# Filling small column tiles over six rounds, making the first matrices in one go with a repeated product, and putting the inverses' endings behind the next products

## The chip, the core and the metric

The kernel runs on one core of a Trainium2 chip. The metric is device time in microseconds (us) of one execution. Engines are named as the profile names them: PE (TensorE, matrix products, with PEld for its weight loads), DVE (VectorE), ACT (ScalarE), POOL (GpSimd) and SP (SyncE, which only issues DMAs here). DMAs are also issued from POOL's and ACT's queues. Each engine works through its own instructions in order; waits between engines are semaphores that the tile framework sets from the tiles that instructions read and write.

## The reference

Two independent computations, joined along the last axis. Part A is an attention layer that goes over 64 segments of 32 positions, each with the 8 memory rows that the segment before it left. Part B, the one that this change touches, is a state space convolution:

```python
dt = jnp.exp(log_dt)[:, None]
logdA = dt * (A_re + 1j * A_im)
P = jnp.exp(logdA[:, :, None] * l[None, None, :])
K = jnp.einsum('dn,dnl,dn->dl', Cc, P, dB).real      # D = 1024 channels, N = 128, L = 2048
Kf = rfft(pad(K, L)); Uf = rfft(pad(u, L))           # length 2 L
y = irfft(Uf * Kf)[:, :, 0:L]
out_B = transpose(y) + u * Dskip
```

Part A, per segment s, with the weights Wq, Wk, Wv (1024 x 32 x 128 each) and Wo:

```python
h = concat([mem, x[:, s*32:(s+1)*32]])
p = softmax(mask(q k^T * scale)); o = (p v) Wo
mem = o[:, :8]; out = o[:, 8:]
```

## The kernel before

Part B comes first and part A after it. Part B has four stages.

**Table rounds.** A loop over `f` from -1 to 16 makes the kernel values K. Sixteen rounds r of channels pass through it; round r is begun in iteration r and ended in iteration r+1. In a round PE makes the exponents (`pa`) and the phases (`ptt`), ACT takes the exponentials (`E0` to `E7`, in a buffer `E`), then the sines (`S`) and cosines (`C`) of both halves, DVE moves phases (`n`), takes absolute values (`b`), negates (`w`) and forms the products `gi` and `gr`, and PE multiplies these into the kernel values (`K`, tile `kp`), which DVE writes into the tile `KxT` (`x`). The order of these steps is a list of words written by hand, `ORDER`, and `LAST` for f = 16; a word with a prime belongs to the round before. ACT changes its table between the exponentials and the sines once per round each way.

Beside the rounds run side operations, at places that the list names: `P`, projections of weights (tile `pro`); `U`, the forward transform of u: PE makes `ups`, ACT copies one as `ua`, DVE forms sum and difference `us` (L974, L975), POOL combines these into `ux` (L979 to L982) and stores it to the DRAM table `Ud` (L983); `M`, transposes of the transform's matrices, `mt`, evicted into `ms` (L946) and stored by POOL to `MId` (L947). A side operation runs in one place and is evicted (`run_evict`) at a later one.

**Columns of turns.** The matrices G of the kernel's spectrum are sines of angles that are products of two small factors, `lhs` (7 rows, 1408 columns) and `rhs` (7 rows, 2048 columns), and a weight factor `wts`. Their transposed columns, `g_l` and `g_r`, are filled in `columns_of_turns` by some forty small instructions of POOL (iota, memset, affine_select) and DVE (shifts, masks, casts), all called ahead of the round f = 3; DVE and POOL read each other's results there. In round 15 `turned_columns` transposes them on PE into tiles `gt` (30 transposes in four groups) in the slots of the side operation `P`, and ACT and DVE copy them to `lhs`, `wts` and `rhs`.

**Passage.** `build` is a generator that makes one block of G in 14 steps: one product and sine for a basis, five pairs of products with a sine each, three products with a copy (the amplitudes, into `amp`), five more pairs with a sine. In f = 16 the step `G0` does nine steps of `build(0, ...)` and `G2` the other five. `weighted` multiplies part of G by the amplitudes on DVE, and `spectrum(b, n)` (L1171) multiplies G with the kernel values `k` in 20 products of 128x256. After the rounds, the last kernel values are stored to the DRAM table `Kd` from `KxT`, in DMAs dealt out to SP and POOL in turn. `make(kc, n)` does steps of the three other blocks.

**Product loop.** For b = 0 to 15, `pointwise(b)` multiplies the spectra of u (`uq`, loaded from `Ud` by SP) by those of the kernel (in PSUM) into `z` and `y` (four multiplies, L1366), then adds and subtracts (L1369, L1370) and writes `Bt` (L1372). It is a generator with a stop behind the multiplies; between its two halves the loop issues the products of spectrum b+1. From b = 4 on, each iteration runs two inverses. An inverse is 32 products into `yp` (and one more of 4 rows for one kind), an eviction by ACT into `yb` (L1438), a multiply of `uu` by `Dsk` and an addition of `yb` on DVE (L1441, L1442) and a DMA of `uu` to the output from ACT's queue (L1443), which is held back in the list `unsent` until a later inverse. The tile `uu` is loaded by SP six inverses ahead, into nine buffers. The product tiles of the spectra, `hps`, have three buffers. Eight inverses are left for a tail behind the loop, in which the resident weights of part A are loaded too.

Part A streams most of its weights (`wst`) from DRAM in every segment.

The lines that set the order around the change:

```python
LAST = ("w0' b0' C0' b1' gi0' C1' G0 gr0' w1' gr1' gi1' K0' K1' G1 x0' x1' G2 M0 G3 m0").split()
for f in range(-1, 17):
    if f == 3:
        columns_of_turns()
```

Of the kernel before, what the change touches and what calls it, by code (L numbers as in the profile page):

```python
# [10 lines left out]
BF16 = mybir.dt.bfloat16  # L11
# [651 lines left out]
def part_b(ctx, tc, u, A_re, A_im, B_re, B_im, C_re, C_im, log_dt, Dskip, out_b, ahead, copies, residents, first_state):  # L663
# [32 lines left out]

    g_l = tabs.tile([128, 14, 7], BF16, name="g_l")
    g_r = tabs.tile([128, 4, 4, 7], BF16, name="g_r")
    par_t = [tabs.tile([128, 8, 128], BF16, name="pt%d" % n_) for n_ in range(2)]
# [222 lines left out]
    tmp = ctx1.enter_context(tc.tile_pool(name="b_tmp", bufs=2))  # L922
    up = ctx1.enter_context(tc.tile_pool(name="b_up", bufs=1, side="right"))
    ctx_p = ctx.enter_context(ExitStack())
    ps_t = ctx_p.enter_context(tc.tile_pool(name="b_pst", bufs=2, space=PSUM))
# [116 lines left out]
    def columns_of_turns():  # L1042

        at = tabs.tile([128, 6], I32, name="g_at")
        for j, (b0, step) in enumerate(((0, 2), (256, 2), (512, 4), (1024, 8), (2048, 16), (0, 2))):
            gp.iota(at[:, j:j + 1], pattern=[[1, 1]], base=b0, channel_multiplier=step)
        atF = tabs.tile([128, 6], F32, name="g_atF")
        v.tensor_copy(out=atF[:], in_=at[:])

        def select(t_, dims, fill, base, cm):  # L1050
            gp.affine_select(out=t_, in_=t_, compare_op=ALU.is_ge, fill=float(fill), base=base, pattern=[[0, n_] for n_ in dims], channel_multiplier=cm)
        for j, fill in ((2, 513), (3, 1025), (4, 2050)):
            select(atF[:, j:j + 1], (1,), fill, -1, 1)
        select(atF[:, 5:6], (1,), 1, 4, -1)
        select(atF[:, 5:6], (1,), 3, 5, -1)
        v.tensor_copy(out=at[:], in_=atF[:])
        hl = tabs.tile([128, 2, 6], I32, name="g_hl")
        v.tensor_scalar(out=hl[:, 0, :], in0=at[:], scalar1=6, scalar2=None, op0=ALU.logical_shift_right)
        v.tensor_scalar(out=hl[:, 1, :], in0=at[:], scalar1=63, scalar2=None, op0=ALU.bitwise_and)
        for i, (lo, n_) in enumerate(((0, 2), (2, 3))):  # L1060
            v.tensor_copy(out=g_l[:, 0:10, lo:lo + n_].rearrange("p (s j) c -> p s j c", s=2),
                          in_=hl[:, i, 0:5].unsqueeze(1).unsqueeze(3).to_broadcast([128, 2, 5, n_]))
            v.tensor_copy(out=g_l[:, 10, lo:lo + n_], in_=hl[:, i, 5:6].to_broadcast([128, n_]))
        gp.memset(g_l[:, 0:11, 5:6], 1.0)
        gp.memset(g_l[:, 0:11, 6:7], 0.25)
        gp.memset(g_l[:, 5:10, 6:7], 0.0)
        pn = tabs.tile([128, 4], I32, name="g_pn")
        gp.iota(pn[:, 0:1], pattern=[[1, 1]], base=0, channel_multiplier=1)
        v.tensor_scalar(out=pn[:, 1:2], in0=pn[:, 0:1], scalar1=1, scalar2=None, op0=ALU.bitwise_and)
        v.tensor_scalar(out=pn[:, 2:3], in0=pn[:, 0:1], scalar1=4, scalar2=None, op0=ALU.logical_shift_right)  # L1070
        v.tensor_scalar(out=pn[:, 3:4], in0=pn[:, 0:1], scalar1=15, scalar2=None, op0=ALU.bitwise_and)
        pnF = tabs.tile([128, 5], F32, name="g_pnF")
        v.tensor_copy(out=pnF[:, 0:4], in_=pn[:])
        gp.memset(g_l[:, 11:14, :], 0.0)
        gp.memset(g_l[:, 11:14, 0:1], 1.0)
        gp.memset(g_l[:, 12:14, 1:2], 2.0)
        gp.memset(g_l[:, 13:14, 2:4], 2.0)
        for i, j in ((0, 1), (1, 2), (2, 4)):
            v.tensor_scalar(out=g_l[:, 11 + i, j:j + 1], in0=pnF[:, 1:2], scalar1=-2.0, scalar2=2.0, op0=ALU.mult, op1=ALU.add)
        select(g_l[:, 11:13, 0:5], (2, 5), 0, -1, 1)  # L1080
        select(g_l[:, 13:14, 4:5], (1, 1), 0, -1, 1)
        gp.memset(g_l[:, 11:13, 5:6], 2.0)
        gp.memset(g_l[:, 12:13, 6:7], 2.0)
        select(g_l[:, 11:13, 5:7], (2, 2), 0, 0, -1)
        kq = tabs.tile([128, 2, 16], I32, name="g_kq")
        gp.iota(kq[:, 0, :], pattern=[[1, 4], [0, 4]], base=0, channel_multiplier=0)
        gp.iota(kq[:, 1, :], pattern=[[0, 4], [1, 4]], base=0, channel_multiplier=0)
        kqF = tabs.tile([128, 2, 16], F32, name="g_kqF")
        v.tensor_copy(out=kqF[:], in_=kq[:])
# [6 lines left out]
        gp.memset(g_r[:, :, :, 5:6], 128.0)  # L1096
        gp.memset(g_r[:, :, :, 6:7], 1.0)

    G = {}

    def turned_columns():

        for i in range(4):
            pt = take([128, 8, 128], BF16, "gt")
            for c in range(8 if i != 1 else 6):
                pe.transpose(out=pt[0:7, c, :], in_=g_l[:, 8 * i + c, :] if i < 2 else g_r[:, 2 * (i - 2) + c // 4, c % 4, :], identity=ident[:])

            def evict(copy, i=i, pt=pt):
                flat = pt[0:7].rearrange("p c n -> p (c n)")
                if i == 0:  # L1110
                    copy(out=G["lhs"][:, 0:1024], in_=flat)
                elif i == 1:
                    copy(out=G["lhs"][:, 1024:1408], in_=flat[:, 0:384])
                    copy(out=G["wts"], in_=flat[:, 384:768])
                else:
                    copy(out=G["rhs"][:, 1024 * (i - 2):1024 * (i - 2) + 1024], in_=flat)
            yield evict

# [147 lines left out]
    for eng, names in ((sc.copy, ON_ACT), (v.tensor_copy, ON_DVE)):  # L1266
        for nm, kind, slot in names:
            evict_of[nm] = (kind, slot, eng)
    LAST = ("w0' b0' C0' b1' gi0' C1' G0 gr0' w1' gr1' gi1' K0' K1' G1 x0' x1' G2 M0 G3 m0").split()
    for f in range(-1, 17):  # L1270
        if f == 3:
            columns_of_turns()
        if f == 15:
# [7 lines left out]
            G.update({0: part_of(g0, 0), "rhs": g0[0:7, 5120:7168], "wts": g0[0:7, 7168:7552], "basis": g0[0:7, 7552:8064], "lhs": k0[0:7, 2560:3968]})  # L1281
            side_ops["P"] = (turned_columns(),)
        if f == 16:
# [3 lines left out]
        for word in ORDER if f < 16 else LAST:  # L1287
            nm, r = word.rstrip("'"), f - word.endswith("'")
            if f == 16 and nm[0] in "GMm" and not word.endswith("'"):
                if nm == "G0":  # L1290
                    for _ in range(9):
                        next(made)
                elif nm == "G1":
                    weighted(0, 0, amp0)
                elif nm == "G2":
                    for _ in made:
                        pass
                    s0 = ps_e.tile([128, 2, 512], F32, name="pa", tag="pa")
# [15 lines left out]
            elif nm in evict_of:  # L1314
                run_evict(*evict_of[nm])
                if f == 15 and nm == "m":
                    run_evict("U", 3, v.tensor_copy)
            elif nm[0] in side_ops:
# [6 lines left out]
            elif 0 <= r <= 15:  # L1325
                table_ops[nm[:-1]](r, int(nm[-1]))
                if f == 15 and nm == "x1":
                    run_side("U", 3)
    for n_, f_ in enumerate(late):
        f_((sy, gp)[n_ % 2])  # L1330
# [95 lines left out]
    def inverse(dq, c, uu, neg, mn):  # L1426
# [11 lines left out]
        sc.activation(out=yb[:], in_=yp, func=ACT.Copy, scale=float(2.0 / PLEN))  # L1438
        while len(unsent) > (1 if len(todo) > 6 else 0):
            unsent.pop(0)()  # L1440
        v.tensor_tensor(out=uu[:], in0=uu[:], in1=Dsk[:, d].unsqueeze(1).to_broadcast([128, 2, DQ]), op=ALU.mult)  # L1441
        v.tensor_tensor(out=uu[:], in0=uu[:], in1=yb[:], op=ALU.add)  # L1442
        unsent.append(lambda: sc.dma_start(out=out_v[r][:, mc:mc + 2, d], in_=uu[:]))  # L1443

# [13 lines left out]
    for b in range(16):  # L1458
# [3 lines left out]
        points = pointwise(b, now)  # L1462
        next(points)
        if b == 0:
            ctx_p.close()
# [46 lines left out]
    for n_ in range(3):  # L1512
        inverse_begin(3, 2 * n_, begun[n_ // 2][:, n_ % 2])
    ctx2.close()
    for n_ in range(8):
        inverses(1)
        for _ in range((9, 5)[n_] if n_ < 2 else 1):
            next(resident, None)
# [161 lines left out]
```

## Time and profile before

| what | us |
|---|---|
| median of 3 runs | 2044.19 (2042.81 to 2046.65) |
| profiled execution | 2047.62 |
| its span in the profile | 2045.9 |
| table rounds end (ACT's last exponential table) | about 424 |
| first multiply of `pointwise(0)` starts | 466.94 |
| product loop in a steady period (b = 4 on) | 13.07 each |
| part A's PE work starts | about 697 |

Mean granted TensorE clock: 0.975. The bytes moved are 588.69 MB, at a mean of 288 GB/s. A row of a timeline has the start, the length, the engine, the line, the operation, output and inputs, and in brackets the engine's idle time before it and the instruction that ended it. A row of a group has the total busy time and the mean of one in ns, then the idle time before the group's instructions and its main releaser. A line number is that of the kernel before. "PEclk" is the granted clock as a share of the full one.

### The profile page before, as it was taken

The page shows a single profiled execution, that of the slowest core. Times are in us where ns is not written, and L with a number is a line of the kernel's source. Part 1 is how long each engine was busy: PE and PEld are TensorE (multiplying, and loading weights), DVE is VectorE, ACT ScalarE, POOL GpSimd, SP SyncE. Part 2 cuts the span into 40 slices and gives each one's busy share as a digit, 9 for nine tenths or more (in the row PEclk, how much of TensorE's full clock was granted, in tenths as well). Part 3 has the DMA queues.
Part 4 walks back from the last instruction along what each step waited for, and adds up shares of the span by engine and source line. Part 5 has one row for each costly group of instructions (what it writes and reads, how often), then busy time and mean ns, then how long its engine had stood idle before and what let it go on. Part 6 is the DMA issues. An engine that isn't in the chain of part 4 may idle for free.

```text
span 2045.9 us, 74541 instructions
## 1 busy us (share of the span) xinstructions
PE 1834.5 (90%) x31928; PEld 1130.4 (55%) x31956; DVE 1411.2 (69%) x3442; ACT 958.1 (47%) x1672; POOL 415.3 (20%) x851
## 2 busy tenths in 40 slices
PE   1698999866999879999999999999999999999998
PEld 1365666644877535555555555555555555555554
DVE  8878999958887346666766667666666666666650
ACT  4887988862222324443444444444434444344430
POOL 2135454442200011111111111111111111111121
PEclk9999999977999979999999999999999999999999
DMA  6787997746446999999999999999999999999991
GB/s 169 185 227 227 274 269 202 200 139 212 158 141 203 316 325 339 340 341 340 344 348 332 339 335 358 344 343 344 350 325 350 342 339 341 345 347 344 345 339 50
DMA packets 348469, 588.69 MB, mean 288 GB/s; under 512 B 109865, under 2 KB 225913, under 8 KB 346089
## 3 DMA queue, kind: packets, MB, share of 16 engines
q1 hardware_dynamic: 294748, 526.35, 76.0%
q10 hardware_dynamic: 44812, 28.26, 4.5%
q0 software_dynamic: 8576, 29.32, 4.0%
q8 instruction: 250, 4.10, 0.8%
q14 instruction: 83, 0.67, 0.1%
HBM read 528.25 MB, written 66.05 MB: 290 GB/s over the span
## 4 chain that ended last, share of the span: by engine, by line
PE 35%; DMA 24%; DVE 4%; issue 1%; ACT 1%; POOL 0%; SPq 0%; POOLq 0%; DVEq 0%; ACTq 0%
PE acc L375 18%; DMA wst<-WD_v 11%; PE pp L488 9%; DMA wst<-WD_o 5%; DMA arena<-PKd 3%; PE pe L625 3%; PE tr L386 2%; DMA wst<-WD_q 2%; DMA wst<-WD_k 2%; PE pv L456 1%; PE pv L460 1%; DVE arena L582 1%; ACT arena L582 1%; PE sc L400 1%; PE tro L588 1%
## 5 line engine op out<-in xcount | busy, mean ns | idle before, releaser
L375 PEld LDWEIGHTS <-a_hT 128*32 128x32 bf16 x12352 | 327.2, 96 | 318.3 <-issue 63.0
L381 ACT CAST arena<-acc 128x512 bf16<-128x512 f32 x384 | 224.7, 585 | 397.6 <-PE acc L375 321.9
L375 PE MATMUL acc<-W,a_hT 128*32 128x512 bf16 x4608 | 334.7, 380 | 2.2 <-issue 1.2
L488 PEld LDWEIGHTS <-arena 128*32 128x32 bf16 x8256 | 216.8, 97 | 86.3 <-issue 62.5
L375 PE MATMUL acc<-wst,a_hT 128*32 128x512 bf16 x2304 | 229.7, 381 | 26.6 <-DMA wst<-WD_v 17.8
L389 POOL COPY arena<-arena 128x128 bf16<-128x128 bf16 x128 | 37.4, 292 | 851.4 <-DMA arena<-PKd 300.3
L296 DVE TENSOR_SCALAR arena<-keep 128x256 int32<-128x256 int32 (+1 forms) x512 | 175.5, 394 | 28.1 <-PE acc L375 26.8
L375 PE MATMUL acc<-gF,a_hT 128*32 128x512 bf16 x2048 | 145.6, 382 | 0.0
L488 PE MATMUL pp<-W_o,arena 128*32 128x256 bf16 x4096 | 139.0, 275 | 6.4 <-DMA W_o<-in_A_Wo_dram 5.1
L168 PE MATMUL pro<-xTl,wsl 128*128 128x512 bf16 x490 | 115.9, 389 | 16.2 <-ACT kst L177 7.9
L415 DVE TENSOR_REDUCE a_mx<-sc 128x4 f32<-128x160 f32 (+1 forms) x192 | 71.6, 373 | 77.5 <-PE sc L403 77.5
L419 ACT ACTIVATE sc<-sc 128x160 f32<-128x160 f32 (+1 forms) x192 | 63.9, 333 | 122.9 <-DVE sc L416 122.1
L503 DVE COPY arena<-tr 128x512 bf16<-128x512 bf16 x64 | 27.2, 425 | 128.3 <-PE tr L386 128.3
L423 DVE TENSOR_REDUCE a_mx<-sc 128x4 f32<-128x160 f32 (+1 forms) x192 | 72.8, 379 | 55.5 <-ACT sc L419 55.1
L1208 ACT ACTIVATE E<-pa 128x648 bf16<-128x648 f32 x128 | 90.9, 710 | 32.2 <-PE pa L1200 27.0
L1423 PE MATMUL yp<-Bt,MI 128*128 128x256 bf16 x680 | 104.6, 273 | 0.7 <-ACT yb L1438 0.7
L450 POOL TENSOR_TENSOR arena<-arena,a_BD 128x128 bf16<-128x128 bf16 x128 | 51.0, 399 | 234.9 <-DVE arena L433 218.5
L168 PEld LDWEIGHTS <-wsl 128*128 128x128 bf16 x512 | 51.1, 100 | 77.7 <-issue 23.3
L582 ACT CAST arena<-pp 128x128 bf16<-128x128 f32 x64 | 17.0, 265 | 161.3 <-DVE arena L582 161.3
L375 PE MATMUL acc<-W_v,a_hT 128*32 128x512 bf16 x1280 | 92.3, 381 | 0.0
L1216 DVE TENSOR_SCALAR nr<-ptt 128x456 f32<-128x456 int16 x128 | 77.3, 624 | 17.7 <-PE ptt L1194 16.0
L386 PEld LDWEIGHTS <-arena 128*128 128x128 bf16 x1024 | 57.8, 98 | 54.5 <-issue 44.9
(311 smaller groups left out, 3866.5 us busy)
## 6 DMA issues: line engine op xcount, KB each, us to landing
wst<-WD_v SPq DMA_DIRECT2D x256, 512.0 KB
wst<-WD_k SPq DMA_DIRECT2D x192, 512.0 KB
wst<-WD_o SPq DMA_DIRECT2D x192, 512.0 KB
wst<-WD_q SPq DMA_DIRECT2D x128, 512.0 KB
Ud<-ux POOLq DMA_DIRECT2D x16, 1024.0 KB, 6.1
uq<-Ud SPq DMA_DIRECT2D x32, 512.0 KB
wsl<-in_A_Wk_dram SPq DMA_DIRECT2D x16, 512.0 KB
wsl<-in_A_Wv_dram SPq DMA_DIRECT2D x16, 512.0 KB
```

What stands on the lines that cost most here:

```text
L168: nc.tensor.matmul(a[:], lhsT=w[:, kc, 128 * j:128 * j + 128], rhs=xTl[:, kc, :, :].rearrange("p s k -> p (s k)"), start=(kc == 0), stop=( ...
L296: nc.vector.tensor_scalar(out=out.bitcast(I32), in0=in_.bitcast(I32), scalar1=0, scalar2=None, op0=ALU.bitwise_or)
L375: nc.tensor.matmul(a[32 * g:32 * g + 32, o_:o_ + rhs.shape[1]], lhsT=hT[:, kc, :], rhs=rhs, start=(kc == 0), stop=(kc == KC - 1), tile_pos ...
L381: nc.scalar.copy(out=q, in_=a[:])
L386: nc.tensor.transpose(out=p[:, hl, :, :].rearrange("p a b -> p (a b)"), in_=q[:, 128 * hl:128 * hl + 128], identity=ident[:])
L415: nc.vector.tensor_reduce(out=m_, in_=x, axis=AX.X, op=ALU.max)
L419: nc.scalar.activation(out=flat(sc, i), in_=flat(sc, i), func=ACT.Exp, scale=scale)
L423: nc.vector.tensor_reduce(out=m_, in_=x, axis=AX.X, op=ALU.add)
L488: nc.tensor.matmul(po[32 * qt:32 * qt + 32, o_:o_ + rhs.shape[1]], lhsT=oT[:, h % 4, (h % 16) // 4, :], rhs=rhs, start=False, stop=(h == 3 ...
L1208: sc.activation(out=T["E", r, e // 4][:, lo:lo + 8 * NE].rearrange("p (i c) -> p i c", i=2), in_=T.pop(("p", r, e))[:, :, 0:4 * NE], func= ...
L1216: v.tensor_scalar(out=T["n", r, e // 4][:, lo:lo + 8 * NT], in0=T.pop(("t", r, e))[:, 0:8 * NT].bitcast(I16)[:, 0:16 * NT:2], scalar1=floa ...
L1423: pe.matmul(yp[:, b, :], lhsT=m_[:, b, cs, kc, :], rhs=Bt[:, kc, j, half, c_, :], start=(kc == 0 and cs == 0 and half == 0), stop=(kc == 3 ...
```

## The change

It has five parts.

1. `g_l`, `g_r` and the small tiles of `columns_of_turns` move from the pool `tabs` to the pool `up`, on the other side of the memory. Tiles allocated after them shift, and so does what later pools lay over the memory of earlier tiles.
2. `columns_of_turns` becomes a generator with six steps, one at the start of each of the rounds f = 1 to 6.
3. `turned_columns` no longer runs in the slots of `P`: a step is called after each of E1 to E6 of round 15, and its copies are issued with the transposes, the left ones on DVE, the right ones on ACT in halves of 512 columns.
4. In `LAST`, `G0` does all fourteen steps of `build(0, ...)`, and PE makes a product of 128x512 into a spare tile, which nothing reads, after each step. The eviction of the last `U` operation, with the POOL work and the store to `Ud` that follow it, moves from the end of round 15 to behind `x1'` of `LAST`.
5. The end of an inverse (the two DVE instructions on `uu`, and the entry in `unsent`) is put into a list, and runs after the next iteration's four multiplies; all of `unsent` is sent after the next inverse's eviction. In the tail it runs right after its inverse.

```diff
-    g_l = tabs.tile([128, 14, 7], BF16, name="g_l")
-    g_r = tabs.tile([128, 4, 4, 7], BF16, name="g_r")
...
     up = ctx1.enter_context(tc.tile_pool(name="b_up", bufs=1, side="right"))
+    g_l = up.tile([128, 14, 7], BF16, name="g_l")
+    g_r = up.tile([128, 4, 4, 7], BF16, name="g_r")
...
     def columns_of_turns():
...
+        gp.memset(g_r[:, :, :, 6:7], 1.0)
+        yield
         v.tensor_copy(out=atF[:], in_=at[:])
...
+            v.tensor_scalar(out=g_l[:, 11 + i, j:j + 1], in0=pnF[:, 1:2], scalar1=-2.0, scalar2=2.0, op0=ALU.mult, op1=ALU.add)
+        yield
         for j, fill in ((2, 513), (3, 1025), (4, 2050)):
             select(atF[:, j:j + 1], (1,), fill, -1, 1)
...
         select(g_l[:, 13:14, 4:5], (1, 1), 0, -1, 1)
+        yield
         rv = g_r[:].rearrange("p k q c -> p (k q) c")
...
+        yield
+        v.tensor_copy(out=at[:], in_=atF[:])
+        v.tensor_scalar(out=hl[:, 0, :], in0=at[:], scalar1=6, scalar2=None, op0=ALU.logical_shift_right)
+        v.tensor_scalar(out=hl[:, 1, :], in0=at[:], scalar1=63, scalar2=None, op0=ALU.bitwise_and)
+        yield
+        for i, (lo, n_) in enumerate(((0, 2), (2, 3))):
...
+        yield
...
-            def evict(copy, i=i, pt=pt):
...
-                    copy(out=G["rhs"][:, 1024 * (i - 2):1024 * (i - 2) + 1024], in_=flat)
-            yield evict
+            flat = pt[0:7].rearrange("p c n -> p (c n)")
+            if i == 0:
+                v.tensor_copy(out=G["lhs"][:, 0:1024], in_=flat)
+            elif i == 1:
+                v.tensor_copy(out=G["lhs"][:, 1024:1408], in_=flat[:, 0:384])
+                v.tensor_copy(out=G["wts"], in_=flat[:, 384:768])
+            else:
+                for h in range(2):
+                    sc.copy(out=G["rhs"][:, 1024 * (i - 2) + 512 * h:1024 * (i - 2) + 512 * h + 512], in_=flat[:, 512 * h:512 * h + 512])
+                    yield
+                continue
+            yield
...
-    LAST = ("w0' b0' C0' b1' gi0' C1' G0 gr0' w1' gr1' gi1' K0' K1' G1 x0' x1' G2 M0 G3 m0").split()
+    LAST = ("w0' b0' C0' b1' gi0' C1' G0 gr0' w1' gr1' gi1' G1 K0' x0' K1' x1' U3 G2 M0 G3 m0").split()
+    steps = columns_of_turns()
     for f in range(-1, 17):
-        if f == 3:
-            columns_of_turns()
+        if 1 <= f <= 6:
+            next(steps)
...
-            side_ops["P"] = (turned_columns(),)
+            turning = turned_columns()
...
-            if f == 16 and nm[0] in "GMm" and not word.endswith("'"):
+            if f == 16 and nm == "U3":
+                run_evict("U", 3, v.tensor_copy)
+            elif f == 16 and nm[0] in "GMm" and not word.endswith("'"):
                 if nm == "G0":
-                    for _ in range(9):
-                        next(made)
+                    spare = ps_t.tile([128, 512], F32, name="ptt", tag="ptt")
+                    for _ in made:
+                        pe.matmul(spare[:], lhsT=ident[:], rhs=MF[:, 0, 0:2].rearrange("p c s n -> p (c s n)"), start=True, stop=True)
                 elif nm == "G1":
                     weighted(0, 0, amp0)
                 elif nm == "G2":
-                    for _ in made:
-                        pass
...
                 run_evict(*evict_of[nm])
-                if f == 15 and nm == "m":
-                    run_evict("U", 3, v.tensor_copy)
...
                     run_side("U", 3)
+                elif f == 15 and nm in ("E1", "E2", "E3", "E4", "E5", "E6"):
+                    next(turning)
...
-        while len(unsent) > (1 if len(todo) > 6 else 0):
+        while unsent:
             unsent.pop(0)()
-        v.tensor_tensor(out=uu[:], in0=uu[:], in1=Dsk[:, d].unsqueeze(1).to_broadcast([128, 2, DQ]), op=ALU.mult)
-        v.tensor_tensor(out=uu[:], in0=uu[:], in1=yb[:], op=ALU.add)
-        unsent.append(lambda: sc.dma_start(out=out_v[r][:, mc:mc + 2, d], in_=uu[:]))
+
+        def ending():
+            v.tensor_tensor(out=uu[:], in0=uu[:], in1=Dsk[:, d].unsqueeze(1).to_broadcast([128, 2, DQ]), op=ALU.mult)
+            v.tensor_tensor(out=uu[:], in0=uu[:], in1=yb[:], op=ALU.add)
+            unsent.append(lambda: sc.dma_start(out=out_v[r][:, mc:mc + 2, d], in_=uu[:]))
+        endings.append(ending)
+
+    endings = []
+
+    def end():
+        while endings:
+            endings.pop(0)()
...
         next(points)
+        end()
...
     ctx2.close()
+    end()
     for n_ in range(8):
         inverses(1)
+        end()
```

More of the change, by code (lines that the diff above doesn't have):

```diff
@@ L1042, in columns_of_turns, with select @@
     def columns_of_turns():
-        at = tabs.tile([128, 6], I32, name="g_at")
+        def select(t_, dims, fill, base, cm):
+            gp.affine_select(out=t_, in_=t_, compare_op=ALU.is_ge, fill=float(fill), base=base, pattern=[[0, n_] for n_ in dims], channel_multiplier=cm)
+        at, pn, kq, hl = (up.tile([128, *dims], I32, name="g_%s" % nm) for nm, dims in (("at", (6,)), ("pn", (4,)), ("kq", (2, 16)), ("hl", (2, 6))))
+        atF, pnF, kqF = (up.tile([128, *dims], F32, name="g_%sF" % nm) for nm, dims in (("at", (6,)), ("pn", (5,)), ("kq", (2, 16))))
@@ L1045, in columns_of_turns @@
         for j, (b0, step) in enumerate(((0, 2), (256, 2), (512, 4), (1024, 8), (2048, 16), (0, 2))):
             gp.iota(at[:, j:j + 1], pattern=[[1, 1]], base=b0, channel_multiplier=step)
[L1047 to L1051, printed above, removed]
+        gp.iota(pn[:, 0:1], pattern=[[1, 1]], base=0, channel_multiplier=1)
@@ new lines, in columns_of_turns @@
+        gp.iota(kq[:, 0, :], pattern=[[1, 4], [0, 4]], base=0, channel_multiplier=0)
+        gp.iota(kq[:, 1, :], pattern=[[0, 4], [1, 4]], base=0, channel_multiplier=0)
+        gp.memset(g_l[:, 0:11, 5:6], 1.0)
+        gp.memset(g_l[:, 0:11, 6:7], 0.25)
+        gp.memset(g_l[:, 5:10, 6:7], 0.0)
+        gp.memset(g_l[:, 11:14, :], 0.0)
+        gp.memset(g_l[:, 11:14, 0:1], 1.0)
+        gp.memset(g_l[:, 12:14, 1:2], 2.0)
+        gp.memset(g_l[:, 13:14, 2:4], 2.0)
+        gp.memset(g_l[:, 11:13, 5:6], 2.0)
@@ new lines, in columns_of_turns @@
+        gp.memset(g_l[:, 12:13, 6:7], 2.0)
+        select(g_l[:, 11:13, 5:7], (2, 2), 0, 0, -1)
+        gp.memset(g_r[:, :, :, 5:6], 128.0)
+        gp.memset(g_r[:, :, :, 6:7], 1.0)
+        yield
+        v.tensor_copy(out=atF[:], in_=at[:])
+        v.tensor_scalar(out=pn[:, 1:2], in0=pn[:, 0:1], scalar1=1, scalar2=None, op0=ALU.bitwise_and)
+        v.tensor_scalar(out=pn[:, 2:3], in0=pn[:, 0:1], scalar1=4, scalar2=None, op0=ALU.logical_shift_right)
+        v.tensor_scalar(out=pn[:, 3:4], in0=pn[:, 0:1], scalar1=15, scalar2=None, op0=ALU.bitwise_and)
@@ L1052, in columns_of_turns @@
+        v.tensor_copy(out=pnF[:, 0:4], in_=pn[:])
+        v.tensor_copy(out=kqF[:], in_=kq[:])
+        for i, j in ((0, 1), (1, 2), (2, 4)):
+            v.tensor_scalar(out=g_l[:, 11 + i, j:j + 1], in0=pnF[:, 1:2], scalar1=-2.0, scalar2=2.0, op0=ALU.mult, op1=ALU.add)
+        yield
         for j, fill in ((2, 513), (3, 1025), (4, 2050)):
@@ L1055, in columns_of_turns @@
         select(atF[:, 5:6], (1,), 3, 5, -1)
[L1056 to L1079, printed above, removed]
         select(g_l[:, 11:13, 0:5], (2, 5), 0, -1, 1)
         select(g_l[:, 13:14, 4:5], (1, 1), 0, -1, 1)
[L1082 to L1089, printed above, removed]
+        yield
         rv = g_r[:].rearrange("p k q c -> p (k q) c")
@@ L1095, in columns_of_turns @@
         v.tensor_scalar(out=rv[:, :, 4], in0=kqF[:, 1, :], scalar1=1.0 / 8, scalar2=0.0, op0=ALU.mult, op1=ALU.add)
-        gp.memset(g_r[:, :, :, 5:6], 128.0)
-        gp.memset(g_r[:, :, :, 6:7], 1.0)
+        yield
[4 more added lines that the diff above has]
+        for i, (lo, n_) in enumerate(((0, 2), (2, 3))):
+            v.tensor_copy(out=g_l[:, 0:10, lo:lo + n_].rearrange("p (s j) c -> p s j c", s=2),
+                          in_=hl[:, i, 0:5].unsqueeze(1).unsqueeze(3).to_broadcast([128, 2, 5, n_]))
+            v.tensor_copy(out=g_l[:, 10, lo:lo + n_], in_=hl[:, i, 5:6].to_broadcast([128, n_]))
+        yield
     G = {}
@@ L1106, in turned_columns @@
                 pe.transpose(out=pt[0:7, c, :], in_=g_l[:, 8 * i + c, :] if i < 2 else g_r[:, 2 * (i - 2) + c // 4, c % 4, :], identity=ident[:])
-            def evict(copy, i=i, pt=pt):
[L1109 to L1115, printed above, removed]
-                    copy(out=G["rhs"][:, 1024 * (i - 2):1024 * (i - 2) + 1024], in_=flat)
-            yield evict
+            flat = pt[0:7].rearrange("p c n -> p (c n)")
[10 more added lines that the diff above has]
+            yield
     def sine_of(out, bank):
```

## The prediction

> **What bounds the kernel now.** I read the busy shares first, then the groups of instructions around each edit, then the timelines of single engines at the four places that the diff touches, and last the waits of the loop that follows. The span is 2045.9 us, the profiled execution 2047.62 us (1.72 outside the span), which is 3.43 above the median of 2044.19. A change of the sum is taken off the median. No engine is full over the whole span, so each stage has to be read by itself:
>
> ```profile
> PE 1834.5 (90%) x31928; PEld 1130.4 (55%) x31956; DVE 1411.2 (69%) x3442; ACT 958.1 (47%) x1672; POOL 415.3 (20%) x851
> ```
>
> The recurrent part fills 697 to 2046 us and is not in the diff. The diff lies in the table rounds (to 424 us), the passage to the products (424 to 473), the product loop (473 to 665) and its tail.
>
> First place, the round in which the columns are filled. Groups on ACT and DVE from 157 to 172 us (the last field is idle time and what ended it):
>
> ```profile
> L1230 ACT ACTIVATE nr<-nr,hp 128x1824 bf16<-128x1824 f32 x2 | 3.5, 1808 | 5.6 <-DVE nr L1227 5.6
> ...
> L1089 DVE CAST g_kqF<-g_kq 128x32 f32<-128x32 int32 x1 | 0.2, 180 | 1.0 <-POOL g_kq L1087 1.0
> L1056 DVE CAST g_at<-g_atF 128x6 int32<-128x6 f32 x1 | 0.2, 172 | 1.0 <-POOL g_atF L1051 1.0
> L1048 DVE CAST g_atF<-g_at 128x6 f32<-128x6 int32 x1 | 0.2, 171 | 1.6 <-POOL g_at L1046 1.6
> ```
>
> DVE and POOL hand small tiles to each other, DVE stands still for 3.6 us of it, and ACT, which sets the pace of the rounds, waits 5.55 us for the cosine's angles behind that.
>
> Second place, the passage. Timelines of ACT, POOL, PE and DVE (start, length, instruction, idle time before it and its end):
>
> ```profile
> 435.09 1.51 ACT L1142 CAST amp<-gf 128x512 bf16<-128x512 f32 x3
> 441.80 2.56 ACT L1120 ACTIVATE g<-gf 128x512 bf16<-128x512 int16 x5 [5.20 <-PE gf L1129]
> ```
>
> ```profile
> 429.47 2.12 POOL L980 TENSOR_TENSOR ux<-us 128x512 f32<-128x512 f32 x1
> 431.55 5.20 POOL L982 TENSOR_TENSOR ux<-us 128x256 f32<-128x256 f32 x4
> 437.16 0.57 POOL L983 DMA_DIRECT2D Ud<-ux  x1 [0.41 <-POOL ux L982]
> 450.16 0.56 POOL L947 DMA_DIRECT2D MId<-ms  x1 [12.43 <-ACT ms L946]
> ```
>
> ```profile
> 441.16 2.31 PE L1129 MATMUL gf<-g,k 7*128 7x256 bf16 x10
> 443.40 4.45 PE L1171 MATMUL pa<-k,g 128*128 128x256 bf16 x20
> 447.64 1.06 PE L942 MATMUL mt<-b_ident,MF 128*128 128x128 bf16 x8
> 448.49 2.76 PE L1171 MATMUL ptt<-k,g 128*128 128x256 bf16 x20
> ```
>
> ```profile
> 444.38 0.96 DVE L1151 TENSOR_TENSOR g<-g,amp 128x1536 bf16<-128x1536 bf16 x1 [2.55 <-ACT g L1120]
> 466.94 1.22 DVE L1366 TENSOR_TENSOR z<-uq,pa 128x1024 f32<-128x1024 f32 x1 [21.60 <-DMA Kd<-KxT]
> ```
>
> The first matrices are made in two parts, 5.20 us apart. Both spectra are ready at 451.2, but the first multiply waits to 466.94, for the kernel table's last stores: its tile z lies in the memory of KxT, which they read.
>
> Third place, the product loop. PE and DVE in one period (13.07 us, 524.64 to 537.71):
>
> ```profile
> 537.71 2.35 PE L1171 MATMUL hps<-k,gF 128*128 128x256 bf16 x20
> 541.28 2.36 PE L1171 MATMUL hps<-k,gF 128*128 128x256 bf16 x20 [1.22 <-DVE y L1366]
> ```
>
> ```profile
> 538.54 0.43 DVE L1442 TENSOR_TENSOR uu<-uu,yb 128x512 bf16<-128x512 bf16 x1 [2.14 <-ACT yb L1438]
> 538.88 1.21 DVE L1366 TENSOR_TENSOR z<-uq,hps 128x1024 f32<-128x1024 f32 x1
> ```
>
> DVE stands before the ending's addition until the inverse is evicted, and the multiplies that free PE's product buffer are queued behind it.
>
> **The change part by part.**
>
> *Columns over six rounds.* ACT's sine tables load at 135.07, 155.04 and 181.64: a round is 19.97, the one with the columns 26.60, 6.6 too long. The same steps come in six pieces, each POOL result read a round later, so the waits go. What is left on DVE is some twenty instructions of 0.15 to 0.25 us, 3.6 us, beside a slack of about 0.46 per round (0.23 before each of two steps waiting on ACT). I leave 0.8 (0 to 2). Gain 5.8, range 4.5 to 6.6.
>
> *Transposes and columns' copies in round 15.* Before, PE does them at 402 to 404 in an idle time that lasts to 412. Now they are queued after E1 to E6. DVE meets the first copy (7x1024, about 0.98 by ACT's row of that shape) after `pa` of E1, which PE starts at 412.12, and the second after E2's eight `ups` products, at about 416.6, ahead of wn, gr1 and gi1 in its order. So gi1, ending at 415.58 before, ends about 421.2; the kernel products that read it stand at 418.17, and go to about 421.3. ACT loses two 0.98 copies and gains four halves between its E evictions. This is a cost of 4 (0.5 if DVE takes the wait in the 1.1 it stands idle later and the rest of the round closes up, 5 if all of it is passed on).
>
> *First matrices in one go, with a repeated product.* ACT's fourteen steps are 2.95 + 1.51 + 2.56 = 7.0 us. From 432.23 they would end at 439.3, where before they end at 444.3. The product after each step is 128x512: at the half clock of 430 to 445 (granted 0.50) about 0.43, beside 0.46 for a step's own two. At 0.9 to 1.0 a step PE is slower than ACT's 0.5. The rows show how long that lasts: PE works without a gap from 443.40, and only the second spectrum (2.76 against 4.45) sees the full clock, some 5 us later. So three steps lie ready in their banks, five more come at 0.96 and six at ACT's 0.5: all made at about 440.7, and the spectra at full clock, 2.2 each instead of 4.45 and 2.76. [...]
>
> *Last eviction of the u-products moved behind x1'.* POOL's additions ran from 427.5 to 436.8, and DVE's big products beside them took up to 2.18 instead of 1.10; four such us on DVE go, so gi1' ends before the matrices do. The price: `us` (1.3) at about 442.5, ux (5.3 without company) to 449, its store issued at 449 where it was 437.16, and MId's store behind it in POOL's queue. The next matrices' amplitude copies on ACT write over what these two stores read. The Ud store takes 6.1, so they start at about 455 and end at 457 (before 455.98).
>
> *z moved off KxT's memory.* With the tiles shifted between the pools, the first multiply waits for the spectra alone: about 445 to 446 instead of 466.94. The next bound is the amplitude copies: weighted(1) can begin at 457 and its second half, after five sines (2.5), ends at 460.7. Before, this ended at 473.4. With the 4 of round 15 it is 464.7: the passage gains **9** net (3 if POOL's chain lands some 6 later, 16 if round 15 costs nothing and the stores land in 3). From there DVE runs without gaps up to 511 in both kernels. The late Kd stores land as before and are read only at b=2, 20 us later.
>
> *Endings behind the next products.* z, y of b now follow Bt of b-1 directly; the endings wait for yb behind them, and who waits for the multiplies after them is Bt, which PE needs an iteration or more later. PE loses 1.39 per period (second spectrum 3.57 after the first, 2.18 if nothing waits) ten times: **13.9**. DVE's own work is 9.3 for the products and 1.57 for the endings, 10.9 against PE's remaining 11.68. Range 8 to 15, since 0.8 of slack is thin. The uu load that reuses a buffer waits for an out store sent no later in the row of inverses than before, so SP's queue is not held longer.
>
> *Tail and start of the recurrent part.* SP's five uu loads from 650.14 hold the resident weights back to 666.37; the store that the last one awaits is now sent one inverse (3.8) earlier. The DMA is full from there to 742, so this counts, if the memory is free. I take **2** (-3 to +4).
>
> Sum: 5.8 + 9 + 13.9 + 2 = 30.7; 2044.2 - 30.7 = 2013.5 (profile: 2047.6 to about 2017).
>
> **The rivals.**
>
> 1. *The endings bring nothing*: DVE stays the bound at 13.07, with waits only shifted from `uu` to Bt. For it: 0.8 of slack. Against it: PE's inverses read Bt of four iterations before. 2013.5 + 13.9 = 2027.4.
>
> 2. *The repeat does not do what it says*: PE stays at half clock, 11 steps at 0.96 end 2.8 later, two spectra at 4.45 cost 4.5 more. For it: the granted clock stood at 0.50 through 15 us in which PE was busy 8.17. About 7 of the 30.7: 2020.5.
>
> 3. *The weights swallow it*: the recurrent part's start is set by 25 MB of loads at 340 GB/s, and if those start no earlier, all is swallowed: 2044. Against it: the DMA's share from 525 to 660 is 0.53, and SP issues by buffers that the loop frees.
>
> 4. *Slower: the recurrent part's period.* With pools and start shifted, its stream may fall otherwise into its weight waits (PE waits 17.8 us in all for wst<-WD_v). 1304 us for 63 segments is 20.7 each; from 0.49 more in each segment the whole gain is lost, at 0.6 (3%) the time is 2051. For it: 24% of the chain that ended last is DMA. Against it: none of that part's instructions is in the diff.
>
> **How the numbers follow.** A measurement of this kernel tells about 0.2%, 4.1 us, from no change. Forecast 0.70, rival 1 0.10, rival 2 0.11, rival 3 0.04, rival 4 0.05. The terms' ends, not all at once, give 2005 to 2022 for the forecast; the range goes on to rival 1, 2005 to 2029, and leaves out rivals 3 and 4. Faster 0.91, same 0.04, slower 0.05.
>
> **What would show it.** Right: the round at 155 is 20 to 21 long; ACT's fourteen steps run without the 5.20 gap, and PE's clock is near 1 when pa's spectrum starts; z of b=0 starts about 20 earlier, weighted(1) only 9 earlier; the period from 525 to 650 is 11.7 and PE has no wait on DVE y there. Wrong: z of b=0 waits on a store, ACT's amplitude copies wait far beyond 461, the period is still 13, or the first segment takes more than 45.

## The result, and the profile after

The changed kernel takes 2022.82 us (median of four runs, 2017.37 to 2029.32), against 2045.42 for the kernel before on the same chip (2042.81 to 2051.64). The ratio is 0.9886, 95% interval 0.9849 to 0.9924: 22.6 us or 1.1% faster, with the interval from 15.5 to 31. That is inside the forecast range and 9 short of the forecast of 2013.5. The profiled execution is one of the faster ones, with a span of 2015.4 (2045.9 before).

Part A, which the diff does not touch, took from 1337 to 1354 us in the profiled executions of this study, so totals scatter by several us. The marks inside part B are much steadier, so the accounting goes by them. The time at which a mark is reached:

| mark | before | after | gained since the mark above |
|---|---|---|---|
| ACT loads the exponential table of round 15 | 410.07 | 404.54 | 5.53 |
| ACT loads the sine table of f = 16 | 423.94 | 422.34 | -3.93 |
| first difference of y and z, b = 0 (behind weighted(1)) | 473.34 | 463.81 | 7.93 |
| first eviction of an inverse (b = 4) | 521.08 | 512.36 | -0.81 |
| last eviction in the loop (b = 15) | 664.07 | 640.58 | 14.77 |
| ACT issues the first load of part A's state | 696.58 | 671.09 | 2.00 |

Together 25.49 at the start of part A; the forecast had 30.7 there. Line numbers after are up to 15 higher.

The columns. Groups on ACT and DVE in the kernel after, from 152 to 172 us and from 80 to 260 us:

```profile
L1231 ACT ACTIVATE nr<-nr,hp 128x1824 bf16<-128x1824 f32 x2 | 3.5, 1800 | 0.0
```

```profile
L1071 DVE CAST g_kqF<-g_kq 128x32 f32<-128x32 int32 x1 | 0.2, 174 | 0.0
L1089 DVE CAST g_at<-g_atF 128x6 int32<-128x6 f32 x1 | 0.2, 164 | 0.0
L1066 DVE CAST g_atF<-g_at 128x6 f32<-128x6 int32 x1 | 0.2, 161 | 0.0
```

The last field, 1.0 to 1.6 for these casts and 5.6 for the cosines before, is zero. ACT loads the sine table at 135.75, 156.21 and 176.18: the long round is gone.

Round 15, DVE and ACT in the kernel after:

```profile
408.65 0.68 DVE L1109 COPY k<-gt 7x1024 bf16<-7x1024 bf16 x1 [3.48 <-PE gt L1106]
409.26 0.61 DVE L1217 TENSOR_SCALAR nr<-ptt 128x456 f32<-128x456 int16 x1
410.91 0.35 DVE L1111 COPY k<-gt 7x384 bf16<-7x384 bf16 x1 [1.04 <-PE gt L1106]
```

```profile
415.53 0.71 ACT L1209 ACTIVATE E<-pa 128x648 bf16<-128x648 f32 x1 [2.20 <-DVE gi L1184]
```

DVE stands for 4.5 us before two small copies, and what is queued behind them (wn, gr1, gi1) reaches E5 on ACT late.

The passage, with ACT, PE, POOL and DVE in turn:

```profile
434.75 0.58 ACT L1143 CAST amp<-gf 128x512 bf16<-128x512 f32 x1 [0.48 <-PE gf L1142]
435.82 0.58 ACT L1143 CAST amp<-gf 128x512 bf16<-128x512 f32 x1 [0.49 <-PE gf L1142]
...
458.87 1.56 ACT L1143 CAST k<-gf 128x512 bf16<-128x512 f32 x3 [4.90 <-DMA MId<-ms]
```

```profile
435.72 0.61 PE L1297 MATMUL ptt<-MF,b_ident 128*128 128x512 bf16 x1
436.26 0.60 PE L1142 MATMUL gf<-g 7*128 7x512 bf16 x1
436.79 0.61 PE L1297 MATMUL ptt<-MF,b_ident 128*128 128x512 bf16 x1
...
444.15 3.88 PE L1172 MATMUL pa<-k,g 128*128 128x256 bf16 x20
```

```profile
451.99 0.56 POOL L983 DMA_DIRECT2D Ud<-ux  x1 [0.41 <-POOL ux L982]
452.59 0.56 POOL L947 DMA_DIRECT2D MId<-ms  x1
```

```profile
448.07 1.22 DVE L1369 TENSOR_TENSOR z<-uq,pa 128x1024 f32<-128x1024 f32 x1 [0.44 <-PE pa L1172]
...
460.52 0.96 DVE L1152 TENSOR_TENSOR gF<-gF,k 128x1536 bf16<-128x1536 bf16 x1 [7.71 <-ACT k L1143]
```

The 5.20 gap on ACT has become a wait of 0.31 to 0.49 before each step that ACT finds not yet made: PE takes 1.07 for a step's product and the repeat together. z of b = 0 waits for its spectrum alone and starts 18.9 earlier, but weighted(1) waits 7.71 for ACT's copies, which wait for the store of MId, issued behind that of Ud.

The loop. Waits before from 525 to 650 us (total, times, longest), then the waits of the kernel after from 512 to 641 us and PE's spectra in it:

```profile
PE hps L1171 <- DVE y L1366: 12.3, 10, 1.2
DVE uu L1442 <- ACT yb L1438: 23.2, 10, 3.3
```

```profile
DVE uu L1447 <- ACT yb L1441: 7.2, 9, 1.1
```

```profile
527.81 4.31 PE L1172 MATMUL hps<-k,gF 128*128 128x256 bf16 x38
539.26 4.53 PE L1172 MATMUL hps<-k,g 128*128 128x256 bf16 x40
```

Both spectra of a b run as one group, without a wait between them (the view of the first begins two products late); PE's wait on DVE y, 12.3 us before, is absent from the list after, and PE is busy for 128.00 of the 128 us from 512 to 640. DVE's wait before the ending's addition is 7.2 where 23.2 stood.

### The profile page after: what moved, and what is told of

Read it like the earlier page. It is cut to its first block, busy times and chain, and to the rows that moved or that the text cites. A ratio compares the mean times of both kernels' runs of the same rounds, so it can differ in the third digit from the quotient of the medians.

```text
span 2015.4 us, 74609 instructions
## 1 busy us (share of the span) xinstructions
PE 1836.9 (91%) x31970; PEld 1130.0 (56%) x31970; DVE 1407.8 (70%) x3443; ACT 959.4 (48%) x1673; POOL 417.7 (21%) x851
## 4 chain that ended last, share of the span: by engine, by line
PE 40%; DMA 21%; DVE 3%; issue 1%; ACT 1%; POOL 0%; SPq 0%; POOLq 0%; DVEq 0%
PE acc L375 23%; DMA wst<-WD_o 8%; PE pp L488 8%; DMA wst<-WD_v 7%; PE pe L625 3%; PE tr L386 2%; DMA wst<-WD_k 2%; DMA arena<-PKd 2%; DMA wst<-WD_q 1%; DVE arena L582 1%; PE pv L456 1%; PE sc L400 1%; PE pv L460 1%; ACT arena L582 1%; PE tro L588 1%
## 5 line engine op out<-in xcount | busy, mean ns | idle before, releaser
L488 PE MATMUL pp<-wst,arena 128*32 128x256 bf16 x1536 | 76.9, 276 | 16.7 <-DMA wst<-WD_o 14.5
```

The source lines that it names most:

```text
L488: nc.tensor.matmul(po[32 * qt:32 * qt + 32, o_:o_ + rhs.shape[1]], lhsT=oT[:, h % 4, (h % 16) // 4, :], rhs=rhs, start=False, stop=(h == 3 ...
```

## The experiments

To compare kernels the stretch from the exponential table of round 15 to part A's first load is used, where no more is said: it leaves out both the start of the execution and part A. It is 286.51 before and 266.55 after. Round 15 alone, from one table to the next, took 17.72 to 18.64 in five executions of the same code, so a difference of less than 1 us in the stretch says little; where it matters, the time from the sine table of f = 16 on is given too. Pools alone, the full operand and the two runs with three repeats were executed once each, and only their marks are used. Ratios are to the kernel before.

**Without the repeat.** The kernel after, with

```diff
-                    spare = ps_t.tile([128, 512], F32, name="ptt", tag="ptt")
                     for _ in made:
-                        pe.matmul(spare[:], lhsT=ident[:], rhs=MF[:, 0, 0:2].rearrange("p c s n -> p (c s n)"), start=True, stop=True)
+                        pass
```

> The kernel after the change, without the repeated 128x512 product. Theory: the repeat makes PE, which stays at half clock, the bound of the fourteen steps (1.07 us a step where ACT needs 0.5), so without it the steps end near 437.5 instead of 442.8, the stores of Ud and MId are issued 5 earlier, and everything from weighted(1) on starts about 5 earlier; z of b=0 starts near 444 if both spectra run at half clock. Rival: the repeat does what it is for, it keeps PE's clock ready for the spectra; without it the spectra take 4.45 and 4.45 and z of b=0 starts no earlier than 448. In time: 5 less than the kernel after, or no less.

The stretch is 259.68, so the repeat costs 6.9, or 7.7 by the time from the sine table on (241.04 against 248.75). ACT's timeline:

```profile
429.76 2.96 ACT L1121 ACTIVATE g<-gf 7x512 bf16<-7x512 int16 x6
432.63 1.51 ACT L1143 CAST amp<-gf 128x512 bf16<-128x512 f32 x3
434.05 2.49 ACT L1121 ACTIVATE g<-gf 128x512 bf16<-128x512 int16 x5
...
451.08 1.56 ACT L1143 CAST k<-gf 128x512 bf16<-128x512 f32 x3 [4.99 <-DMA MId<-ms]
```

The fourteen steps run without a gap. Counted from the sine table, they end 5.8 earlier than with the repeat, the kernel products that PE has queued behind the last repeat start 6.5 earlier, Ud's store is issued 6.5 earlier (at 444.93), and z starts 7.0 earlier (at 440.51). The gain is larger than the 5 expected, and the spectra are not slower either: the first took 3.00, part of it at the full clock (0.88 in the mean of 438 to 440), where it takes 3.88 with the repeat. The time is 2014.82, ratio 0.984 (0.9806 to 0.9874).

**Transposes at their old place.** The kernel after, with the old `turned_columns` and its slots:

```diff
-            turning = turned_columns()
+            side_ops["P"] = (turned_columns(),)
...
-                elif f == 15 and nm in ("E1", "E2", "E3", "E4", "E5", "E6"):
-                    next(turning)
```

> The kernel after the change, with the transposes and the columns' copies put back into the slots of the side operation P as in the kernel before. Theory: DVE's waits for the transposes (3.48 and 1.04 us) hold gr1, gi1 and E5 of round 15, so the sine table of f=16 is loaded about 3.9 earlier (near 418.4 instead of 422.3) and all that follows is 3.9 earlier. Rival: the passage is bound by the stores of Ud and MId and by POOL's queue, not by the round's end, and less than 1 of it comes through.

From the exponential to the sine table it is 13.86 us, as before (13.87), where the kernel after has 17.80. The stretch is 262.95, so 3.6 of the 3.9 come through. Time 2017.40, ratio 0.9852 (0.9833 to 0.987).

**Endings alone.** The kernel before, with the last part of the diff and nothing else.

> The kernel before with only the inverses' endings put behind the next products. Theory: PE's wait on DVE y goes, the period falls from 13.07 to 11.6 and part A's PE work starts about 15 earlier than 696.6; the time is about 15 less than before. Rival: the resident weights' loads set the start of part A, and less than 5 is left of it.

The stretch is 269.50, 17.0 shorter: 14.8 of it between the first eviction in the loop and the last (128.21 where it took 142.99), and 2.0 in the tail. Time 2031.07, ratio 0.9918 (0.9899 to 0.9936).

**Columns over six rounds alone.** The kernel before, with

```diff
+    steps = columns_of_turns()
     for f in range(-1, 17):
-        if f == 3:
-            columns_of_turns()
+        if 1 <= f <= 6:
+            next(steps)
```

and the generator of the diff, its tiles left in `tabs`.

> The kernel before with only the columns spread over six rounds (tiles, transposes and all else as before). Theory: the exponential table of round 15 is loaded 5.5 earlier (404.5 instead of 410.07), the passage is otherwise as before, and all of it comes through: part A's PE work starts 5.5 earlier. Rival: the stores of Kd, for which z of b=0 waits, are paced by the DMA queues and start no earlier, so that z stays near 467 and the gain is lost there.

The exponential table of round 15 is loaded at 404.54 and part A's first load issued at 691.05: 5.53 earlier at both, with the stretch between at 286.51 as before. z starts at 461.04, so the stores of Kd moved along. Ratio 0.9966 (0.9944 to 0.9988).

**Pools alone.** The kernel before, with `g_l`, `g_r` and the small tiles allocated in `up`.

```diff
-    g_l = tabs.tile([128, 14, 7], BF16, name="g_l")
+    g_l = up.tile([128, 14, 7], BF16, name="g_l")
```

> The kernel before with only the column tiles moved to the other pool. Theory: the wait of z of b=0 for the stores of Kd goes, z starts near 449.5 to 451 when the spectrum is done, weighted(1) follows ACT's amplitude copies, and the first y-z difference starts near 460 instead of 473.3; part A starts 12 to 14 earlier. That is more than the whole passage gained in the kernel after (7.9 from the sine table on), so the rest of that passage's changes costs 5. Rival: without the earlier matrices the wait is only replaced by one for the stores of Ud and MId, and it gains less than 8.

DVE's timeline:

```profile
446.78 1.22 DVE L1366 TENSOR_TENSOR z<-uq,pa 128x1024 f32<-128x1024 f32 x1 [2.54 <-PE pa L1171]
...
454.96 0.96 DVE L1151 TENSOR_TENSOR gF<-gF,k 128x1536 bf16<-128x1536 bf16 x1 [2.90 <-ACT k L1142]
```

The wait for Kd's stores is gone, the first difference of y and z is at 458.19, and the stretch is 273.06: **13.5 shorter**. The move of the tiles alone gives more than the passage of the kernel after gained with all its parts (7.93). ACT's copies are not held here: Ud's store was issued at 436.06, long before them.

**Three parts together.** The kernel before with pools, columns and endings; transposes, first matrices and the last u-eviction as before, no repeat.

> The kernel before with three parts of the change: the column tiles in the other pool, their filling over six rounds, and the inverses' endings behind the next products; the transposes, the first matrices and the last eviction of the u-products as in the kernel before, no repeat. Theory: the parts measured by themselves add: 13.4 (pools) and 17.0 (endings) from the exponential table of round 15 to part A's PE start, so that stretch is 256 instead of 286.5, and the table itself comes 5.8 earlier by the columns; the kernel is about 10 faster than the kernel after, and the other two parts of the change cost those 10. Rival: without the earlier matrices the gains overlap in the passage, the stretch is 262 or more, and the other parts are worth something once the pools are moved.

255.87 against the expected 256: the parts add. Time 2011.75, ratio 0.983 (0.98 to 0.9859). So the two remaining parts of the change cost 10.7 in the kernel after.

**Both costs taken out.** The kernel after, without the repeat and with the old transposes.

> The kernel after without the repeated product and with the transposes at their old place. Theory: the two costs lie in different stages (the steps of the first matrices, and round 15) and add: part A's PE work starts 8.2 + 4.6 = 12.8 earlier than in the kernel after, near 658.3. Rival: both end in the same wait of ACT's amplitude copies for the stores of Ud and MId, and the sum is nearer to 9. The time is 10 to 13 less than the kernel after.

The stretch is 256.16, 10.4 less than after: the two costs add (6.9 and 3.6). The expected 12.8 had been read from marks that contain the start of the execution, which differs by some 2 us from run to run. Time 2010.88, ratio 0.9825 (0.98 to 0.9849).

**The last u-eviction back at the end of round 15**, on top of that:

```diff
-    LAST = ("... x1' U3 G2 M0 G3 m0").split()
+    LAST = ("... x1' G2 M0 G3 m0").split()
...
                 run_evict(*evict_of[nm])
+                if f == 15 and nm == "m":
+                    run_evict("U", 3, v.tensor_copy)
```

> As the run before it, and the last eviction of the u-products put back to the end of round 15. Theory: the store of Ud is issued some 10 to 15 earlier and MId's store no longer stands behind it in POOL's queue, so ACT's amplitude copies of the next matrices start about 3 earlier; POOL's additions slow DVE's products again (2.18 instead of 1.10), which costs z of b=0 2 to 4 but is hidden by that wait. Net 0 to 3 earlier. Rival: the slower DVE products delay the kernel products and all behind them, and it is 2 to 4 later.

254.30, 1.9 shorter (2.6 from the sine table on). Ud's store is issued at 430.10 instead of 440.46, and ACT's copies no longer wait for a store. Counted from the sine table, z starts 1.5 later, behind DVE products that took up to 2.22 instead of 1.12, without consequence. This version has the lowest median: 2004.68, ratio 0.9788 (0.9757 to 0.982), clear of the kernel after, while its interval overlaps those of the two runs above. It differs from the three parts together in the first matrices alone, made in one go and without the repeat: against 255.87 that is worth 1.6 (2.5 from the sine table on).

**Why does PE stay at half clock?** First the repeat with a full stationary operand in place of the identity:

```diff
-                        pe.matmul(spare[:], lhsT=ident[:], ...
+                        pe.matmul(spare[:], lhsT=MF[:, 1, 0, 0], ...
```

> The kernel after with the repeated product's stationary operand changed from the identity to 128x128 values of the transform's matrix MF; same size and place. Theory: the clock did not rise in 12 us of gapless work because the products there keep few cells of the array at work (7 rows, and an identity that is zero off its diagonal); with a full operand the granted clock rises within 3 to 5 us and the steps fall from 1.07 to about 0.55, so they end near 438.5 and z of b=0 starts about 4 earlier. Rival: the operand's values do not matter, the clock stays at 0.50 up to the spectra and nothing changes by more than 0.5.

The clock is 0.50 up to the spectra, a step still 1.07, the stretch 266.38 against 266.55: the values do not matter here. Then three repeats in each step, first with the identity and then with the full operand:

> The kernel after with three repeated products in each step instead of one. Theory: what holds the clock down is the share of PE's time that full products have (half of it in the kernel after); with three quarters the clock rises within some 5 us, and a step then takes 0.86: the steps end near 445 (2 later than in the kernel after). Rival: small products between full ones hold it down at any such share; each step takes 2.1 at half clock and they end near 454, 11 later.

> The kernel after with three repeated products in each step, and with 128x128 values of the matrix MF in place of the identity as their stationary operand. Theory: the identity's zeros and the small share of full products were both needed to hold the clock down; with three quarters of PE's time in products of a full operand it rises within about 5 us of the first step, a step then takes 0.86, and the steps end near 443 to 445. Rival: neither matters, the clock stays at 0.50 until the steps are over, 11 steps at 1.93 end near 452 as with three products of the identity.

Both stay down. The stage row of the first of the two (length, then PE, PEld, DVE, ACT and POOL busy, granted clock, DMA share, GB/s):

```profile
432.00:450.00 18.00, 18.00 (x45) 3.85 (x45) 4.09 (x6) 6.17 (x11) 0.00 (x0) 0.50 0.00 1
```

Steps take 1.93 and end at 452.05 and 449.97 (the second execution reached the sine table 2.1 earlier); the stretch grows to 276.43 and 277.30. Finally, 24 such products in the idle time ahead of the steps, none in them, on top of the version with the lowest median (2004.68):

```diff
+                    for n_, _ in enumerate(made):
+                        for _ in range(24 if n_ == 2 else 0):
+                            pe.matmul(spare[:], lhsT=MF[:, 1, 0, 0], ...
```

> As the run with the repeat left out, the transposes at their old place and the last u-eviction at the end of round 15, and now 24 products of 128x512 into a spare tile in the 6.7 us in which PE waits for the first sine, none after it. Theory: the clock stays up through the idle time, the products of the steps and the two spectra (3.40 and 2.35 there) run at the full clock, and part A starts 1 to 2 earlier than in that run. Rival: the clock falls again during the steps, whose products are small (7 rows), before the spectra come; nothing is gained, and up to 1 is lost where the products run past the first sine.

```profile
418.00:424.00 6.00, 5.88 (x29) 2.47 (x27) 4.55 (x6) 5.73 (x5) 3.77 (x3) 1.00 0.45 178
424.00:428.00 4.00, 1.54 (x7) 0.59 (x7) 4.00 (x3) 4.00 (x7) 4.00 (x4) 1.00 0.00 0
430.00:436.00 6.00, 4.25 (x140) 3.09 (x139) 5.98 (x9) 2.19 (x5) 0.59 (x2) 0.50 0.46 180
```

The clock holds through the filler and the idle time behind it (1.00 to 428), and is lost in the steps (0.50 from 430 on) before the spectra begin at 434.43; the first of them takes 4.45. The rival held: from the sine table on it takes 239.41 against 239.70 without the filler.

## Why the prediction was right, and where it was off

The sign and the range held, and so did the mechanism of every term but one; the sum at part A's start was 5.2 too large, and that one step accounts for most of it. The forecast's own terms ended at 2022; the measured median, 2022.82, lies just beyond them, in the part of the range that was added for rival 1, which did not come. Of the signs that were to show it right, one failed: PE's clock stood at 0.50, not near 1, when pa's spectrum started at 444.15.

*Columns*: forecast 5.8, measured 5.53, alone and in the whole. That the two agree to the digit is chance, since the mark contains the start of the execution: it lies at 401.87 to 404.54 in the eleven profiled executions with the columns spread and at 408.21 to 410.07 in the three without, and the means are 5.6 apart.

*Transposes in round 15*: forecast -4, measured -3.93 by the mark and -3.6 by taking it out. It went as argued: DVE waits in order for the transposes (3.48 and 1.04), and gi1, E5 and the kernel products come late.

*First matrices in one go*: this is the step that failed. It had three steps ready in their banks, "five more come at 0.96 and six at ACT's 0.5", the rest of the way on a clock that rises after 5 us of gapless work. All eleven ran at 1.07 and half clock, so the steps took 12.6 us from ACT's first sine instead of 8.5. Rival 2, to which 0.11 was given, came true in its mechanism, and its 2020.5 is nearer to the result than 2013.5. Its price of about 7 was made up otherwise than it came: 2.8 for the steps and 4.5 for the spectra, where the steps took 4.1 more than the forecast and the spectra, at 3.88 and 2.35, only 1.8. That the run without the repeat gave 6.9 to 7.7 is another comparison, and its nearness to 7 is luck. The evidence was in the view: in the row from which the 5 us were read, the work without a gap was a spectrum. Before 443.40, in 2.3 us of 7-row products, and all through 430 to 445, the clock had not moved from 0.50.

*Passage*: forecast 9 with round 15's 4 taken off, measured 7.93 - 3.93 = 4.0. The chain was the forecast one, us, ux, Ud, MId, ACT's copies, weighted(1), but begun late by the steps: the copies started at 458.87, where the forecast's 455, moved by the other two terms, gives 453.2. Of these 5.7, us was 4.1 late, as much as the steps; POOL's additions and the landing of the stores took the rest. The pools alone give 13.5, nearly the 13 that the forecast had for the passage without round 15; so the making in one go with its repeat and the moved u-eviction, counted as parts of that gain, added nothing to it in the kernel after. Without the repeat, and with the eviction at its old place, the making in one go was worth 1.6. In the forecast's z term, "about 445 to 446", the effect of the memory was right, and the gain that was to come on top from the earlier matrices was not there.

*Endings*: forecast 13.9, measured 14.77 in the loop. The period is PE's, which is busy for 128.00 of the 128 us from 512 to 640: DVE's slack of 0.8 was enough, and rival 1 is out.

*Tail*: forecast 2, measured 2.00, and 2 again with the endings alone. That the weights could start earlier because an out store is sent one inverse earlier fits SP's row: the weights follow 2.9 after the eviction of the loop's next to last inverse (636.71 to 639.60), where before it was 6.1 (660.26 to 666.37), behind the eviction after it. That this alone is the cause was not tried.

*Part A*: rivals 3 and 4 did not come. What reached its start reached the end within its own scatter. The 22.6 of the medians and the 25.5 of the marks are not told apart by these runs.

## What to carry to other kernels

When a tile of a new stage lies over one that DMAs still read, the stage waits for the DMAs (z for 21.60 us in the kernel before); moving some small tiles to another pool was worth 13.5 us here, while the reordered transposes and first matrices that came with it cost 10.7. An engine that takes its work in order, as DVE does here (in the kernel before its multiplies stood behind 23.2 us of waits for the endings' `yb`), should do first what the next stage needs to be fed, and put endings that wait for other engines behind that: it was worth 14.8 us in the loop. Filler work for a clock has to be priced at the clock that it is given, and it must be shown to raise it: here it doubled the time of the steps between which it stood, from about 0.5 us to 1.07.

## What the runs showed of the hardware

PE's clock did not come back by being busy. In the kernel after, PE worked without a gap from 430.91 to 444.15 at 0.50, with three repeats for 18 us and more at 0.50, at about half to three quarters of the time in 128-row products (0.53 of a step's 1.07 us, 1.40 of 1.93), whether the stationary operand was an identity or full. In these runs it came back 0.8 to 4.6 us after the kernel products, which the spectra follow, had begun (453.56 after 452.74 with three repeats, 447.30 after 442.70 in the kernel after).

The traces of the two kernels show where it changed. In the kernel before it was 0.50 from 428.85 to 449.33, 1.00 to 456.15 and 0.50 to 476.63; in the kernel after 0.50 from 426.82 to 447.30, 1.00 to 454.13 and 0.50 to 467.78. Both lost it behind a stretch in which PE had 7-row products alone, though the profile calls PE busy in them: for 4.14 of the 4.97 us from 451.18 to 456.15 in the kernel before, for 3.01 of the 3.54 us from 450.59 to 454.13 in the kernel after. With the filler ahead of the steps it was 1.00 up to 428, 0.68 in the mean of 428 to 430 and 0.50 from 430 to 438, with 7-row products alone on PE from 426.04 to 430.84. This is read off the traces afterwards; no run was made to test it, and none had full products alone between the steps' place and the spectra from the half clock on. How much full work in how long a time raises the clock or holds it was not shown.
